# First-layer weights in two transfers of 2 KB rows, keys' powers on GpSimd, and a last transposition ahead of its logits

## The chip, the cores and the metric

The kernel runs on one core of one Trainium2 chip. A core has a matmul engine (TensorE, PE in the profile, with its weight loads listed as PEld), VectorE (DVE), ScalarE (ACT), GpSimd (POOL) and SyncE (SP). In this kernel SP issues nearly all transfers between HBM and the on-chip memory, and 16 DMA engines carry them out. The metric is the time of one execution in microseconds of device time; lower is better. The profile is one execution recorded by the hardware profiler.

## The reference

The first part is a linear attention with decay over q, k and v of shape (4, 8, 768, 64). It is computed in blocks of 64 positions with a running state per head:

```python
for b in range(nb):
    intra = np.einsum('bhic,bhjc->bhij', qb, kb) * Dmask[None]
    intra = np.einsum('bhij,bhjd->bhid', intra, vb)
    inter = np.einsum('bhid,bhde->bhie', qb * lam_pow[None], kv_state)
    out[:, :, sl] = intra + inter
    kb_dec = kb * rev_pow[None]
    kv_state = lam_block[None, :, None, None] * kv_state + np.einsum('bhsd,bhse->bhde', kb_dec, vb)
```

`Dmask`, `lam_pow` and `rev_pow` are powers of one decay per head. The second part is a soft mixture of experts over the 3072 rows x of that output (512 wide), with 8 experts of 4 slots each:

```python
logits = x @ phi                       # 3072 x 32
d = softmax of logits over the rows    # dispatch
slot_input = d.T @ x                   # 32 slots x 512
h = np.maximum(slot_input[e] @ w1[e], 0.0)   # 512 x 1024 per expert
slot_out[e] = h @ w2[e]                      # 1024 x 512 per expert
c = softmax of logits over the slots   # combine
return c @ slot_out
```

All data are float32. The two weight tensors have 16.8 MB each.

## The kernel before, in words

**Chunks.** The 3072 rows are worked through in T = 24 chunks of 128 rows (6 to a batch element), in a Python loop that writes out every instruction. Each engine runs its own instructions in the order written; a helper records every operation, so that the profile puts all of them on line 52, and one tells them apart by tile names. For chunk t:

- `scores(t)`: PE multiplies keys by queries into the banks `sc0` and `sc1`; DVE multiplies by the decay `mask` into `at`.
- `recall(t)`: PE multiplies the running state `st` by the decayed queries `qs` into the banks `xa` and `xb`.
- `turn_k(t + 1)`: for chunks whose natural-order keys are not loaded, PE transposes `kT` of the next chunk and ACT copies it to `kn`.
- `natural(t - 1)`: PE transposes the finished chunk `xt` into `tr`, ACT copies it to `x`.
- `attend(t)`: PE adds `at` times v into `xa` and `xb`, which are copied to `xt`; then ACT swaps the halves of the next chunk's v into `vs`.
- `state(t)`: PE multiplies the decayed keys `kd` by v into `kv`; DVE adds it to the decayed state.
- `decay_q(t + 1)` and `decay_k(t + 1)`: POOL makes `qs` and `kd` for the next chunk. `kd` needs the keys' powers `kp`.

Every fourth chunk adds the logits of four finished chunks (`logits`, bank `gl`, with a running maximum and an exponential `e` on ACT) and, a chunk later, their contribution to the slot inputs (`slots`, into `acc`).

**Loads.** SP issues the loads in program order. At chunk t it issues qT and kT of chunk t + 2, then as many first-layer tiles as a fixed pace gives (`load_early`; tile `slab`, 128 partitions x 2 x 512), then vN and, where wanted, kN of chunk t + 2. The chunk loads have 256 KB each and go round 10 buffers; a slab has 512 KB, one row of 4 KB per partition, and there are 35 slab buffers: 32 for the first layer w1, and the first ones of w2 (`w2p`, two rows of 2 KB per partition). The rest of w2 is loaded where buffers of the chunk phase come free (`w2t`, 256 KB) and into used slabs (`w2p`). Program order puts kT of chunk 3 behind 2 slabs, kT of chunk 12 behind 16, and kT of chunk 21 behind 30.

**Start.** DVE builds `mask` by scans; in chunk 0 ACT swaps v (`swap_v(0)`), copies the powers out of the mask (`key_powers`), and PE runs a few warm-up matmuls on a tile of zeros (into `dp`).

**The bridge.** After the last chunk, `attend(23)` leaves `xt` in two halves, one copied by ACT and one by DVE. The logits of that chunk (`pr`, bank `sc0`) are then multiplied on PE, DVE takes their maximum (`mx`, `nm`), ACT takes the weight `wgt` of what came before (tile `alpha`) and the exponentials `el` (tile `e`), POOL makes `selw` from the weight, and PE transposes `e`. The last chunk is also transposed to natural order (`tr`, copied to `xl`, tile `x`), and `slots` of the last group is done. All of it goes into the slot inputs (`si`, bank `xb`), and with that the expert layers start: `first(0)`, `first(1)` with the slabs, then `second` with w2, between whose parts the output is combined and stored.

The pace at which slabs are issued is set by these lines:

```python
asked = sum(3 + loaded(x) for x in range(min(t + 3, T)))
want = max(sent, min(NSLAB, (AHEAD + (t + 1) * PACE - 10 * asked) // 20))
load_early(want - sent)
```

Of the kernel before, what the change touches and what calls it, by code (L numbers as in the profile page):

```python
# [8 lines left out]
F32 = mybir.dt.float32  # L9
F32R = mybir.dt.float32r  # L10
AF = mybir.ActivationFunctionType
# [3 lines left out]
P = 128  # L15
B, H, S, DH = 4, 8, 768, 64
NB = S // P
T = B * NB
HP = H // 2
D = H * DH  # L20
# [8 lines left out]
HD = D // 2  # L29
# [7 lines left out]
def loaded(t):  # L37

    return t == 0 or t % NB in (2, 4)
# [18 lines left out]
def decay_attn_soft_moe(  # L58
# [13 lines left out]
    pe, dve, act, pool, sp = (InOrder(tc, x) for x in (nc.tensor, nc.vector, nc.scalar, nc.gpsimd, nc.sync))  # L72
# [5 lines left out]
    keep = ctx.enter_context(tc.tile_pool(name="keep", bufs=4))  # L78
    small = ctx.enter_context(tc.tile_pool(name="small", bufs=2))
# [5 lines left out]
    def bank(tag):  # L85
        return SC.get(tag) or ps.tile([P, 512], F32, tag=tag, name=tag)
# [7 lines left out]
    def load_chunk(t, which=(0, 1, 2, 3)):  # L94
        srcs = (qT, kT, vN, kN)
        for i in which:
            if i == 3 and not loaded(t):
                continue
            tl = loads.tile([P, 512], F32, tag="ld", name="ld")
            sp.dma_start(out=tl, in_=srcs[i][t])  # L100
            IN[t, i] = tl
# [13 lines left out]
    def load_one(pool_, tag, bufs):  # L115
        Q, f, q = late.pop()
        t_ = pool_.tile([P, 512], F32, tag=tag, name="w2t", bufs=bufs)
        sp.dma_start(out=t_, in_=w2[4 * Q + q, f])
        wt["w2", Q, q, f] = t_

    def load_two():

        (Q, f, q), _ = late.pop(), late.pop()
        t_ = slabs.tile([P, 2, 512], F32, tag="slab", name="w2p")
        sp.dma_start(out=t_, in_=w2[4 * Q + q:4 * Q + q + 2, f].rearrange("e p d -> p e d"))
        for i in range(2):
            wt["w2", Q, q + i, f] = t_[:, i, :]

    def load_early(n):
        for _ in range(n):  # L130
            if early:
                _, Q, kc, q = early.pop()
                t_ = slabs.tile([P, 2, 512], F32, tag="slab", name="slab")
                sp.dma_start(out=t_, in_=w1[4 * Q + q, kc])
                wt["w1", Q, q, kc] = t_
            else:
                load_two()
# [9 lines left out]
    def warmup(n):  # L147
        for _ in range(n):
            pe.matmul(out=wps[:, 0:P], lhsT=warm[:, P:2 * P], rhs=warm[:, P:2 * P], start=True, stop=True)
# [5 lines left out]
    ident = const.tile([P, P], F32, name="ident")  # L155
# [16 lines left out]
    mask = work.tile([P, 2, HP, P], F32, tag="mask", name="mask")  # L172
    for hh in range(2):
        for hp in range(HP):
            x = hh * HP + hp

            dve.tensor_tensor_scan(
                out=mask[:, hh, hp, :],
# [21 lines left out]
    kp = small.tile([P, 2, HP, 1], F32, tag="kp", name="kp", bufs=1)  # L200
    kpow = kp.rearrange("p a b o -> p (a b) o")

    def key_powers():
        act.copy(out=kp[:, :, 0:2], in_=mask[:, :, 0:2, P - 1:P])
        for i in range(2):
            act.copy(out=kp[64 * i:64 * i + 64, :, 2:HP], in_=mask[64 - 64 * i:P - 64 * i, :, 2:HP, P - 1:P])

    CN = const.tile([P, T, SL], F32, name="CN")
    acc = const.tile([P, D], F32, name="acc")
# [4 lines left out]
    def load_phi():  # L214

        sp.dma_start(out=e.rearrange("p (k s) -> p k s", k=4), in_=phi)
# [10 lines left out]
    AT, XT, X, ST, QS, KD = {}, {}, {}, {}, {}, {}  # L227
# [192 lines left out]
    def weights(raw=True):  # L420
        dp = bank("dp")
        pe.transpose(dp[:, 0:P], e, ident)
        if raw:
            pe.transpose(dp[:, P:2 * P], L, ident)
        dve.tensor_copy(out=d, in_=dp[:, 0:P])
        return dp[:, P:2 * P]
# [57 lines left out]
    for t in range(T):  # L484
        if t + 2 < T:
            load_chunk(t + 2, (0, 1))
# [4 lines that stand above are left out]
        sent = max(sent, want)  # L491
        if t + 2 < T:
            load_chunk(t + 2, (2, 3))
        if t == 1:
            load_phi()

        for _ in range((2, 4, 3)[t - T + 3] if t >= T - 3 else 0):
            load_one(*ld1)
        if t == T - 1:
            load_one(work, "kd", 1)  # L500
            load_one(work, "kn", 1)
        last = t == T - 1

        asks = t // 4 - 1 if t > 0 and t % 4 == 0 else G - 1 if last else None
        sums = t // 4 - 1 if t > 4 and t % 4 == 1 else None
        scores(t)
        if t == 0:
            swap_v(0)
            key_powers()
            warmup(2)  # L510

        if t % 4 == 3 or t % 4 == 0:
            next(sm, None)
        if t == T - 1:
            next(sm, None)
        opens = t % NB == 0
        if t == 0:
            decay_k(0)
            powers()
            decay_q(1)  # L520
        recall(t)
        if sums is not None:
            sm = slot_softmax(sums, weights())
        if t > 0:
            if not opens:
                turn_k(t + 1)
            natural(t - 1)
        if sums is not None:
            next(sm)
        if asks is not None:  # L530
            ask = logits(asks)
            next(ask)
        if last:
            next(ask)

            phi4 = [
                work.tile([P, 2, 4, SL], F32, tag=tg, name="phi4", bufs=n) for tg, n in (("dec", 1), ("st", 2))
            ]
            for i in range(2):
                two = phi_sb[:, 2 * i:2 * i + 2].rearrange("p (a o) s -> p a o s", o=1)  # L540
                pool.tensor_copy(out=phi4[i], in_=two.broadcast_to([P, 2, 4, SL]))
        if opens and t > 0:

            state(t)
        attend(t)
        if t == 0:
            state(0)
            turn_k(1, "tr")
        if last:
            weights(raw=False)  # L550
            cm = bank("kv")
            pe.matmul(out=cm[:, 0:4], lhsT=blk_, rhs=gm, start=True, stop=True)
            dve.tensor_reduce(out=own, in_=cm[:, 0:4], axis=AX.X, op=ALU.min)
        if t == 0:
            dve.tensor_reduce(out=sel, in_=ident.rearrange("p (g s) -> p s g", g=4), axis=AX.X, op=ALU.add)
            for Q in range(2):
                rows = bass.AP(tensor=ident.tensor, offset=ident.offset + 16 * Q, ap=[ident.ap[0], [36, 4], [1, NR]])
                dve.tensor_reduce(out=own2[:, Q:Q + 1], in_=rows, axis=AX.XY, op=ALU.add)
            dve.tensor_reduce(out=gsel, in_=ident.rearrange("p (g s) -> p g s", g=4), axis=AX.X, op=ALU.add)
        if opens and t > 0:  # L560
            turn_k(t + 1)
        if t > 0:
            decay_q(t + 1)
        if not opens:
            state(t)
        decay_k(t + 1)
        if asks is not None and not last:
            next(ask)
        if sums is not None:
            slots(sums)  # L570
        if t == 2:
            place_phi()
        if t == 3:
            pool.tensor_copy(out=blk, in_=sel.rearrange("p (o s) -> p o s", o=1).broadcast_to([P, 4, SL]))
# [4 lines left out]


    negm = run["m"]
    pr = bank("sc0")
    for hp in range(HP):
        pe.matmul(
            out=pr[:, 0:P],
# [7 lines left out]
    dve.tensor_reduce(out=mx, in_=pr, axis=AX.X, op=ALU.max)  # L593
    new = small.tile([P, 1], F32, tag="nm", name="nm")
    dve.scalar_tensor_tensor(out=new, in0=mx, scalar=-1.0, in1=own, op0=ALU.mult, op1=ALU.min)
    tr = bank("tr")
    for hp in range(HP):
        pe.transpose(tr[:, hp * P:(hp + 1) * P], XT[T - 1][:, hp, :], ident)
    xl = keep.tile([P, D], F32, tag="x", name="x", bufs=5)
    act.copy(out=xl[:, 0:HD], in_=tr[:, 0:HD])  # L600
    dve.tensor_copy(out=xl[:, HD:D], in_=tr[:, HD:D])
    wgt = small.tile([P, 1], F32, tag="alpha", name="alpha")
    act.activation(out=wgt, in_=negm, func=AF.Exp, bias=new, scale=-1.0)
    el = e
    rs = small.tile([P, 1], F32, tag="rs", name="rs")
    act.activation(out=el, in_=pr, func=AF.Exp, bias=new, scale=1.0, accum_out=rs)
    selw = small.tile([P, SL], F32, tag="selw", name="selw", bufs=1)
    pool.tensor_scalar(out=selw, in0=sel, scalar1=wgt, scalar2=None, op0=ALU.mult)
    for half in range(2):
# [7 lines left out]
    for first_, (w_, x_) in ((True, (selw, acc)), (False, (dn, xl))):  # L617
        for kc in range(4):
            pe.matmul(
                out=si[SL * kc:SL * kc + SL, 0:P],  # L620
# [242 lines left out]
```

## Time and profile before

| | |
|---|---|
| median of 3 runs | 167.2 us (166.39 to 169.53) |
| the profiled execution | 166.92 us, span 165.1 us |
| busy: PE, PEld, DVE, ACT, POOL | 145.9, 104.5, 93.1, 81.0, 65.8 us |
| moved by DMA | 61.56 MB, mean 373 GB/s |
| first matmul of the first expert layer | 116.15 us |
| last matmul on the chain that ended last | about 155.6 us |

The span runs from the first to the last recorded instruction. The profile gives each engine's busy time; the waits (which instruction stood idle, and what released it); the timeline (start, duration, engine, operation, output and inputs, how many are merged in one line, and in brackets the idle time before it with its releaser); the DMA issues (kind, count, KB, and the time from issue to landing); and the DMA queues (packets, MB, and the share of 16 engines' time). "issue" in brackets means that the engine waited for nothing that the profile shows. PE is busy in most of the span, and the 16 DMA engines are busy in nearly all of it.

### The profile page before, as it was taken

The page shows a single profiled execution, that of the slowest core. Times are in us where ns is not written, and L with a number is a line of the kernel's source. Part 1 is how long each engine was busy: PE and PEld are TensorE (multiplying, and loading weights), DVE is VectorE, ACT ScalarE, POOL GpSimd, SP SyncE. Part 2 cuts the span into 40 slices and gives each one's busy share as a digit, 9 for nine tenths or more (in the row PEclk, how much of TensorE's full clock was granted, in tenths as well). Part 3 has the DMA queues.
Part 4 walks back from the last instruction along what each step waited for, and adds up shares of the span by engine and source line. Part 5 has one row for each costly group of instructions (what it writes and reads, how often), then busy time and mean ns, then how long its engine had stood idle before and what let it go on. Part 6 is the DMA issues. An engine that isn't in the chain of part 4 may idle for free. (4 is left out here: it accounts for less than half of the span.)

```text
span 165.1 us, 6357 instructions
## 1 busy us (share of the span) xinstructions
PE 145.9 (88%) x2633; PEld 104.5 (63%) x2633; DVE 93.1 (56%) x218; ACT 81.0 (49%) x203; POOL 65.8 (40%) x93
## 2 busy tenths in 40 slices
PE   6788977999999979998999999998999999999800
PEld 6567866678796857686767888775233345456600
DVE  4984433458475546449265848586118799345800
ACT  3445645457365646565475746542010698333800
POOL 2188592227766107658322766710000285000000
PEclk9999999999999999999999999999999999999965
DMA  5999999999999999999999999998999999998895
GB/s 171 350 406 404 414 405 410 410 406 408 401 349 395 412 409 404 414 329 354 396 396 402 391 383 377 333 311 325 358 397 408 409 401 408 400 370 301 310 384 199
DMA packets 32012, 61.56 MB, mean 373 GB/s; under 512 B 3056, under 2 KB 9328, under 8 KB 31984
## 3 DMA queue, kind: packets, MB, share of 16 engines
q1 hardware_dynamic: 31840, 61.16, 98.7%
q8 instruction: 21, 0.34, 0.8%
q14 instruction: 7, 0.06, 0.1%
q10 hardware_dynamic: 144, 0.01, 0.1%
HBM read 54.86 MB, written 6.29 MB: 370 GB/s over the span
## 5 line engine op out<-in xcount | busy, mean ns | idle before, releaser
L52 DVE TENSOR_TENSOR at<-sc,mask 128x512 f32<-128x512 f32 x48 | 30.9, 685 | 13.0 <-PE sc L52 12.6
L52 POOL TENSOR_TENSOR qs<-ld,qpow 128x512 f32<-128x512 f32 x20 | 25.6, 1279 | 2.0 <-POOL kd L52 1.3
L52 ACT COPY x<-tr 128x512 f32<-128x512 f32 (+1 forms) x24 | 13.9, 579 | 22.7 <-PE tr L52 22.7
L52 PE MATMUL sc<-ld 64*64 64x128 f32 (+1 forms) x768 | 22.7, 252 | 2.4 <-issue 2.4
L52 PEld LDWEIGHTS sc<-ld 64*64 64x64 f32 x768 | 18.9, 134 | 9.0 <-issue 3.4
L52 ACT COPY vs<-ld 64x256 f32<-64x256 f32 x48 | 19.4, 403 | 5.1 <-DMA ld<-vN 4.3
L52 POOL TENSOR_TENSOR dec<-st,qpow 128x256 f32<-128x256 f32 x16 | 9.9, 621 | 24.8 <-DVE st L52 24.8
L52 POOL TENSOR_TENSOR kd<-kn,kp 128x512 f32<-128x512 f32 x11 | 11.5, 1043 | 15.2 <-ACT kn L52 15.2
L52 DVE TENSOR_TENSOR st<-dec,kv 128x256 f32<-128x256 f32 x16 | 6.7, 420 | 16.9 <-PE kv L52 15.6
L52 PE MATMUL tr<-ident,xt 128*128 128x128 f32 x96 | 15.3, 281 | 0.0
L52 PE MATMUL xa<-qs,st 64*64 64x128 f32 x160 | 13.4, 277 | 1.5 <-issue 1.0
L52 PE MATMUL kv<-ld,kd 128*64 128x64 f32 x320 | 13.2, 223 | 0.8 <-POOL kd L52 0.8
L52 PE MATMUL xb<-qs,st 64*64 64x128 f32 x160 | 13.7, 279 | 0.0
L52 PEld LDWEIGHTS kv<-ld,kd 128*64 128x64 f32 x320 | 12.0, 138 | 1.7 <-POOL kd L52 1.1
L52 POOL TENSOR_TENSOR kd<-ld,kp 128x512 f32<-128x512 f32 x9 | 9.6, 1068 | 6.1 <-ACT kp L52 6.1
L52 PEld LDWEIGHTS tr<-ident,xt 128*128 128x128 f32 x96 | 10.6, 141 | 2.1 <-issue 1.9
L52 ACT COPY kn<-kv 128x512 f32<-128x512 f32 x10 | 5.9, 585 | 11.9 <-PE kv L52 11.9
L52 PE MATMUL xa<-at,ld 128*64 128x128 f32 x96 | 10.4, 295 | 1.1 <-DVE at L52 1.1
L52 PEld LDWEIGHTS xa<-qs,st 64*64 64x64 f32 x160 | 9.0, 133 | 2.2 <-issue 1.3
L52 PE MATMUL xa<-at,vs 128*64 128x128 f32 x96 | 9.6, 273 | 0.3 <-issue 0.3
L52 PE MATMUL xb<-at,vs 128*64 128x128 f32 x96 | 9.6, 273 | 0.0
L52 PE MATMUL xb<-at,ld 128*64 128x128 f32 x96 | 9.5, 274 | 0.0
(152 smaller groups left out, 265.4 us busy)
## 6 DMA issues: line engine op xcount, KB each, us to landing
slab<-w_x SPq DMA_DIRECT2D x32, 512.0 KB, 6.8
w2p<-w_x SPq DMA_DIRECT2D x20, 512.0 KB, 9.2
ld<-qT SPq DMA_DIRECT2D x24, 256.0 KB, 5.9
ld<-kT SPq DMA_DIRECT2D x24, 256.0 KB, 5.9
ld<-vN SPq DMA_DIRECT2D x24, 256.0 KB, 6.8
w2t<-w_x SPq DMA_DIRECT2D x24, 256.0 KB, 5.3
y<-o SPq DMA_DIRECT2D x24, 256.0 KB, 3.5
ld<-kN SPq DMA_DIRECT2D x9, 256.0 KB, 5.8
```

Source lines behind the costliest of these rows:

```text
L52: return self._tc.keep_in_program_order(f(*args, **kwargs))
```

## The change

1. Each first-layer tile is loaded by two transfers of 256 KB, one for each half of the row of a partition (2 KB each), instead of one of 512 KB with rows of 4 KB. The order among the loads is kept.
2. The three small copies that gather the keys' powers go from ACT to POOL, and 4 instead of 2 warm-up matmuls run in chunk 0.
3. In the last chunk, DVE's copy of the logits to `L` and its update of `lsum` (the second step of `logits`) come behind `attend` instead of ahead of it.
4. After the last chunk, its four transpositions and the two copies to `xl` come ahead of its logits instead of behind their maximum; the exponentials `el` come ahead of the weight `wgt` on ACT.

```diff
@@ load_early
                 t_ = slabs.tile([P, 2, 512], F32, tag="slab", name="slab")
-                sp.dma_start(out=t_, in_=w1[4 * Q + q, kc])
+                for i in range(2):
+                    sp.dma_start(out=t_[:, i], in_=w1[4 * Q + q, kc][:, i])
                 wt["w1", Q, q, kc] = t_
@@ key_powers
-        act.copy(out=kp[:, :, 0:2], in_=mask[:, :, 0:2, P - 1:P])
+        pool.tensor_copy(out=kp[:, :, 0:2], in_=mask[:, :, 0:2, P - 1:P])
         for i in range(2):
-            act.copy(out=kp[64 * i:64 * i + 64, :, 2:HP], in_=mask[64 - 64 * i:P - 64 * i, :, 2:HP, P - 1:P])
+            pool.tensor_copy(out=kp[64 * i:64 * i + 64, :, 2:HP], in_=mask[64 - 64 * i:P - 64 * i, :, 2:HP, P - 1:P])
@@ the loop over chunks
             key_powers()
-            warmup(2)
+            warmup(4)
...
         if last:
-            next(ask)
 ...
             state(0)
             turn_k(1, "tr")
         if last:
+            next(ask)
             weights(raw=False)
@@ after the loop
     negm = run["m"]
+    tr = bank("tr")
+    for hp in range(HP):
+        pe.transpose(tr[:, hp * P:(hp + 1) * P], XT[T - 1][:, hp, :], ident)
+    xl = keep.tile([P, D], F32, tag="x", name="x", bufs=5)
+    act.copy(out=xl[:, 0:HD], in_=tr[:, 0:HD])
+    dve.tensor_copy(out=xl[:, HD:D], in_=tr[:, HD:D])
     pr = bank("sc0")
...
     dve.scalar_tensor_tensor(out=new, in0=mx, scalar=-1.0, in1=own, op0=ALU.mult, op1=ALU.min)
-    tr = bank("tr")
-    for hp in range(HP):
-        pe.transpose(tr[:, hp * P:(hp + 1) * P], XT[T - 1][:, hp, :], ident)
-    xl = keep.tile([P, D], F32, tag="x", name="x", bufs=5)
-    act.copy(out=xl[:, 0:HD], in_=tr[:, 0:HD])
-    dve.tensor_copy(out=xl[:, HD:D], in_=tr[:, HD:D])
-    wgt = small.tile([P, 1], F32, tag="alpha", name="alpha")
-    act.activation(out=wgt, in_=negm, func=AF.Exp, bias=new, scale=-1.0)
     el = e
     rs = small.tile([P, 1], F32, tag="rs", name="rs")
     act.activation(out=el, in_=pr, func=AF.Exp, bias=new, scale=1.0, accum_out=rs)
+    wgt = small.tile([P, 1], F32, tag="alpha", name="alpha")
+    act.activation(out=wgt, in_=negm, func=AF.Exp, bias=new, scale=-1.0)
```

## The prediction

> **What bounds the kernel now.** I read the page's busy times, the DMA issues, the chain that ended last, then the waits of SP and of the weight loads, and the timelines around the lines that change.
>
> ```profile
> PE 145.9 (88%) x2633; PEld 104.5 (63%) x2633; DVE 93.1 (56%) x218; ACT 81.0 (49%) x203; POOL 65.8 (40%) x93
> q8 instruction: 21, 0.34, 0.8%
> slab<-w_x SPq DMA_DIRECT2D x32, 512.0 KB, 6.8
> ld<-kT SPq DMA_DIRECT2D x24, 256.0 KB, 5.9
> w2t<-w_x SPq DMA_DIRECT2D x24, 256.0 KB, 5.3
> 116.15 1.07 PE gl L52 x8
> ```
>
> The last row is the chain's first matmul of the first expert layer. From there the chain is PE, piece upon piece without a wait, until 152.1 us; then come the last copies and stores. So the end moves with the moment at which the first layer starts, and an edit counts by what it does to the 24 chunks before 116 us or to the bridge at 111 to 116 us.
>
> In the chunks PE is nearly full, yet it stops in the middle of runs of equal matmuls:
>
> ```profile
> 23.03 0.30 PEld L52 LDWEIGHTS sc<-ld 64*64 64x64 f32 x12 [1.11 <-issue]
> 29.22 0.42 PEld L52 LDWEIGHTS sc<-ld 64*64 64x64 f32 x16 [1.43 <-issue]
> 60.40 0.70 PEld L52 LDWEIGHTS gl<-xt,phi_sb 128*32 128x32 f32 x27 [1.24 <-issue]
> 78.74 0.13 PEld L52 LDWEIGHTS xa<-qs,st 64*64 64x64 f32 x1 [1.28 <-issue]
> q8 instruction: 1, 0.02, 5.5%
> ```
>
> Nothing that the profile shows releases these. The queue row is of the stretch 26.7 to 27.7 us: in it one block of a program was fetched, in 5.5% of 16 engines for 1.0 us = 0.9 us, and PE went on 1.5 us after it, at 29.22. The page counts 2 x 2633 PE instructions and 21 blocks, 251 to a block. I read the stalls as PE at the end of a block with the next one not there. If a block is asked for when PE enters the one before (my inference), the block fetched from 26.7 us was asked for at 23.03 and stood 3.7 us in line, behind what SP had issued.
>
> How much stands in line is set by SP, which issues a transfer only when an earlier one has landed:
>
> ```profile
> 9.11 0.33 SPq L52 DMA_DIRECT2D ld<-kT  x1
> ld<-kT SPq DMA_DIRECT2D x1, 256.0 KB, 6.6
> 15.75 0.33 SPq L52 DMA_DIRECT2D ld<-vN  x1
> SPq L52 <- DMA slab<-w_x: 10.9, 15, 0.9
> ```
>
> This kT lands at 9.11 + 6.6 = 15.7; the vN issued right then is the eighth transfer after it. So eight are in flight, whatever their size, and splitting a slab puts fewer bytes in line.
>
> **The change part by part.**
>
> *The split, as DMA work.* The first two rows are of 26.7 to 27.7 us, where slabs alone are moved, the third of 132 to 138 us, where all rows have 2 KB, the fourth of 20.6 to 21.7.
>
> ```profile
> DMA packets 108, 0.42 MB, mean 416 GB/s; under 512 B 8, under 2 KB 8, under 8 KB 107
> q1 hardware_dynamic: 107, 0.40, 99.2%
> q1 hardware_dynamic: 1251, 2.41, 104.4%
> q1 hardware_dynamic: 229, 0.42, 100.5%
> ```
>
> A 4 KB packet takes 16 x 1.0 x 0.992 / 99 = 160 ns. A 2 KB packet takes 16 x 6 x 1.044 / 1179 = 85 ns without the small ones. A slab has 128 of the first; two halves have 256 of the second: (170 - 160) x 128 / 16 = 0.08 us more per slab, 2.6 us for 32. By the mixed stretch a 2 KB packet takes 16 x 1.1 x 1.005 / 201 = 88 ns: 0.13 us per slab, 4.1 us in all. I take 0.08, from the longer stretch. SP issues 32 more transfers at about 0.33 us, 11 us of its own time, while it waits for landings anyway.
>
> Does a later load stop PE? The tightest places are the transpositions of kT for chunks 3, 12 and 21:
>
> ```profile
> 15.81 0.41 PE L52 MATMUL kv<-ident,ld 128*128 128x128 f32 x2 [0.63 <-DMA ld<-kT]
> 47.39 0.48 SPq L52 DMA_DIRECT2D ld<-kT  x1
> ld<-kT SPq DMA_DIRECT2D x1, 256.0 KB, 7.1
> 55.56 0.42 PEld L52 LDWEIGHTS kv<-ident,ld 128*128 128x128 f32 x4 [0.17 <-issue]
> 88.34 0.42 SPq L52 DMA_DIRECT2D ld<-kT  x1
> ld<-kT SPq DMA_DIRECT2D x1, 256.0 KB, 5.6
> 95.56 0.31 PEld L52 LDWEIGHTS kv<-ident,ld 128*128 128x128 f32 x3 [0.17 <-issue]
> ```
>
> Chunk 3: PE waits already, and 2 slabs stand ahead: +0.16 us, at once. Chunk 12: landed at 54.5, used at 55.56, margin 1.1, against 16 slabs x 0.08 = 1.3. Chunk 21: landed at 93.9, used at 95.56, margin 1.6, against 30 x 0.08 = 2.4. The DMA engines have slack to give back where SP stood waiting for a buffer:
>
> ```profile
> 45.00:50.00 5.00, 5.00 (x118) 4.45 (x118) 3.19 (x10) 3.31 (x11) 2.86 (x3) 1.00 0.96 348
> 70.00:75.00 5.00, 5.00 (x112) 4.25 (x104) 2.93 (x6) 2.67 (x7) 3.11 (x4) 1.00 0.94 335
> 75.00:80.00 5.00, 3.97 (x96) 3.29 (x96) 3.41 (x8) 2.19 (x6) 3.66 (x5) 1.00 1.01 371
> 135.00:140.00 5.00, 5.00 (x99) 2.99 (x92) 4.85 (x12) 4.85 (x13) 3.38 (x9) 1.00 1.05 408
> ```
>
> The last column is GB/s. The fourth row is a full stretch, of 2 KB rows alone. Against its 408 the first lost 5 x 60 / 408 = 0.7 us, the others 0.9 and 0.45. So the loads could be 0.7 us earlier by chunk 12 and 2.1 by chunk 21.
>
> *The split, as a shorter line.* Eight transfers of 256 KB take what the w2t take, 5.3 us to land, against 5.9 to 6.8 now; I put the line 1.1 us shorter. That taken off the first three stalls leaves 0.0, 0.3 and 0.1 us, a gain of 1.1 + 1.1 + 1.1 = 3.3. The fourth falls in the stretch 75 to 80 us, where the engines weren't full, so the line was short already; I leave it whole. But what is late next is the loads. PE can be ahead by 1.1 + 0.7 - 1.3 = 0.5 us at chunk 12, and by 1.6 + 2.1 - 2.4 = 1.3 at chunk 21, if the slack is given back; a PE that is ahead frees its buffers earlier, so it is. After chunk 21 no kT is as near its use. I take the 1.3 us. The bounds for the split: all four stalls gone, a gain of 5.1; or the line unchanged and all DMA work at its upper price on the path, a loss of 4.1.
>
> The Trainium skill ("Runtime: NRT & Kernel Launch", section on instruction fetch mechanics) says that instructions come in blocks of 16 KiB, which its sequencer fetches by a DMA queue of its own, and that crossing a boundary is mostly hidden. The trace agrees on the size (0.34 MB in 21 blocks) and not on the hiding: 1.11 to 1.43 us are shown. By that sentence the stalls would be something else and the gain nothing.
>
> *Keys' powers.*
>
> ```profile
> 7.13 0.61 ACT L52 COPY kp<-mask 128x4 f32<-128x4 f32 x3
> 7.82 1.26 POOL L52 TENSOR_TENSOR kd<-ld,kp 128x512 f32<-128x512 f32 x1 [6.06 <-ACT kp L52]
> 9.76 1.27 POOL L52 TENSOR_TENSOR qs<-ld,qpow 128x512 f32<-128x512 f32 x1 [0.68 <-DVE qpow L52]
> L52 POOL COPY d<-ident 128x64 f32<-128x64 f32 x2 | 0.4, 236 | 0.0
> ```
>
> ACT's three copies, 0.61 us, stand behind its swap of v. POOL waits for them (6.06 us) with nothing else to do, and would need up to 3 x 236 ns = 0.7 us, as they are smaller than that row's: the decayed keys start earlier by what ACT spends on the swap, less 0.1. But POOL's next step waits for DVE's powers until 9.76 in any case, and chunk 3 waits for its load. So 0; without this cover it would be 0.1 slower to 0.8 faster. The two extra warm-up matmuls lie where PE waits for DVE's first `at`, and shift the block ends by a few instructions: 0.
>
> *The bridge.*
>
> ```profile
> 111.21 0.29 DVE L52 COPY L<-gl 96x128 f32<-96x128 f32 x1
> 111.77 1.13 PE L52 MATMUL sc<-xt,phi 128*128 128x128 f32 x8
> 113.37 0.37 ACT L52 COPY x<-tr 128x256 f32<-128x256 f32 x1 [1.75 <-PE tr L52]
> 113.83 0.36 ACT L52 ACTIVATE e<-sc,nm 128x128 f32<-128x128 f32 x1
> 114.03 0.37 POOL L52 TENSOR_SCALAR selw<-sel,alpha 128x32 f32<-128x32 f32 x1 [5.55 <-ACT alpha L52]
> 115.12 0.32 PE L52 MATMUL xb<-acc,selw 128*32 128x128 f32 x4 [0.45 <-DVE dn L52]
> ```
>
> Four transpositions ahead of the eight logits put these 4 x 1.13 / 8 = 0.55 us later in PE's queue. About 0.3 is made good: DVE's part of `xt` no longer stands behind the copy of `L` (0.29). Against the rest, `x` is copied while the logits run, so that ACT is free for `e` when the new maximum comes, and does it ahead of the weight's exponential: `e` some 0.1 us earlier than 113.83. DVE has no copy of `x` left between the maximum and its two `acc` updates. The weight comes after `e`, so `selw` ends near 113.73 + 0.36 + 0.36 + 0.37 = 114.8 (the weight's exponential taken as long as `e`), and PE goes on near 114.9 instead of 115.12. I take -0.2 us; -0.5 if `selw` isn't last, +0.3 if the logits' delay stays.
>
> **Sum.** The 0.16 at chunk 3 is within the 2.4 of the later margin and isn't added. -1.3 - 0.2 = -1.5 us against the profiled execution's 166.9 (a span of 165.1 and 1.8 around it): 165.4. The median of the runs shown, 167.2, is 0.3 above it, so 165.7. A measurement of this kernel can tell about 2%, 3.3 us, from no change.
>
> **Rivals.**
>
> *The line isn't shorter.* The fetch queue may be served between loads, and the stalls have another cause. For it: the 1.28 us stall stands where few slabs were in flight. Against it: the fetch at 26.7 us, 3.7 after the stall that should have triggered it. Then PE keeps its stalls, SP's waits hide the 2.6 us, chunk 3 costs 0.16 and the bridge gives 0.2: 167.2. Chance 0.30. The Trainium skill ("DMA: Bandwidth & Descriptors", section on queues, rings and completion order) has each DMA engine take turns between queues at every packet, which speaks for this rival.
>
> *Loads become the bound (slower).* The halves' source rows lie 4 KB apart, which the trace shows for no load. If a slab costs c more, chunk 21 is pushed by 30c against 1.6 + 2.1 = 3.7 us: it decides from c = 0.12. By the mixed stretch's 0.13 this is 30 x 0.13 - 3.7 = +0.2 us. At twice that, 0.25, it is +3.8, or 171.0, and slower by 2%. Nothing in the rows has such a price, so the middle: c = 0.19, +2.0, 169.2. Chance 0.13, half of it beyond 2%.
>
> *The stalls go whole.* If the loads have more slack than I found, the 3.3 us count, with the bridge's 0.2: 167.2 - 3.5 = 163.7; with the fourth stall, 162.4. For it: the three stretches with slack come after chunk 10 and the price of a slab is small. Against it: chunk 12's 0.5 us. Chance 0.14.
>
> **Numbers.** The forecast has 0.43, with 164.5 to 166.7 as its own range. Range 163.3 to 168.6: it leaves out a third of the whole-gain case and most of the slow one. 2% is reached below 163.9 and above 170.5. Faster by over 2%: most of the 0.14 and a little of the forecast, 0.17. Slower: 0.08. Within: 0.75.
>
> **What would show it.** Slab halves of 256 KB landing in about 5.3 us, and ld in the same; PEld's waits for issue on `sc`, `xa` and `gl` down by 2 us or more; new PE waits for ld near chunks 9 to 12; the first `kd` starting ahead of 7.82; the logits' exponential ahead of the weight's and some 0.1 us earlier against the first logit matmul's old place. I am wrong if the stalls keep their length, or if windows at 10 to 45 us fall well under 400 GB/s.

## The result, and the profile after

The changed kernel takes 168.87 us (median of 20 runs, 165.98 to 173.04), the kernel before 166.8 (20 runs, 164.47 to 172.53): 1.0122 of it, with an interval of 1.0082 to 1.0162. That is slower, by 2.07 us at the medians, where 1.5 us of gain was forecast. Executions over 1.5% above the fastest of their kernel are left out of each ratio, so that it need not be the quotient of the medians; the profiled ones of the changed kernel, of the split alone, of the rows of 2 KB and of the even and odd partitions are among those left out. The profiled execution of the changed kernel took 169.25 us (span 167.5).

First, of the changed kernel, the issues of slabs and kT (count, KB, us to landing), and from the chain the first matmul of the first layer.

```profile
slab<-w_x SPq DMA_DIRECT2D x64, 256.0 KB, 5.5
ld<-kT SPq DMA_DIRECT2D x24, 256.0 KB, 5.3
118.48 1.07 PE gl L52 x8
```

The first layer starts at 118.48 us in place of 116.15. From there to the end it is 169.25 - 118.48 = 50.77 us, and before 166.92 - 116.15 = 50.77. So all of the loss was made ahead of the first layer, as the prediction's first step has it. The windows from 8 us to that start, of before and then of after, split it (PE busy is the second number, the last two are the DMA share and GB/s):

```profile
8.00:116.15 108.15, 100.40 (x2165) 81.00 (x2161) 62.71 (x149) 58.83 (x153) 57.40 (x64) 1.00 1.02 386
```
```profile
8.00:118.48 110.48, 101.25 (x2168) 82.08 (x2164) 62.60 (x150) 59.09 (x153) 56.46 (x64) 0.98 1.03 380
```

PE stands idle for 110.48 - 101.25 = 9.23 us against 7.75 before, 1.48 more, and it is busy 0.85 us longer, at a mean clock of 0.98. What it waits for has changed. Waits of 8 to 96 us, before and after (sum, count, longest), of the matmuls (PE) and of the weight loads (PEld):

```profile
PE sc L52 <- issue: 2.4, 3, 1.3
PE xa L52 <- issue: 1.3, 2, 1.0
PE gl L52 <- issue: 1.1, 1, 1.1
PEld sc L52 <- issue: 3.2, 5, 1.4
PEld xa L52 <- issue: 3.1, 10, 1.3
PEld gl L52 <- issue: 2.3, 7, 1.2
```
```profile
PE kv L52 <- DMA ld<-kT: 3.8, 2, 2.0
PE kv L52 <- issue: 0.7, 1, 0.7
PE sc L52 <- issue: 0.2, 1, 0.2
PEld xa L52 <- issue: 1.4, 7, 0.3
PEld gl L52 <- issue: 1.0, 6, 0.2
PEld sc L52 <- issue: 0.8, 4, 0.3
```

The stalls that the prediction puts down to program blocks, up to 1.4 us each, are gone from `sc`, `xa` and `gl`: what the weight loads still wait there is at most 0.3 us. One of 0.7 us stands on `kv`, at 84.19 us. The matmuls' idle time without a visible cause falls from 2.4 + 1.3 + 1.1 = 4.8 us to 0.9. In its place PE waits for kT, 3.8 us instead of one wait of 0.6, and 0.9 more just behind 96 us. The timeline of after at chunks 3, 15 and 21:

```profile
9.90 0.33 SPq L52 DMA_DIRECT2D ld<-kT  x1
16.79 0.81 PE L52 MATMUL kv<-ident,ld 128*128 128x128 f32 x4 [2.03 <-DMA ld<-kT]
71.07 0.63 PE L52 MATMUL kv<-ident,ld 128*128 128x128 f32 x4 [1.77 <-DMA ld<-kT]
96.69 0.52 PE L52 MATMUL kv<-ident,ld 128*128 128x128 f32 x3 [0.92 <-DMA ld<-kT]
```

The loads are late, and SP shows that it is mostly not for want of a buffer. Its waits over the whole span, before and after: buffers come free when POOL is done with a chunk's keys (`kd`) or PE with its matmuls (`kv`), and SP waits for those far less; for the landing of a slab it waited 10.9 us in 15 waits before.

```profile
SPq L52 <- POOL kd L52: 10.4, 7, 1.8
SPq L52 <- PE kv L52: 9.1, 9, 1.8
```
```profile
SPq L52 <- DMA slab<-w_x: 16.7, 50, 1.8
SPq L52 <- PE kv L52: 2.4, 7, 0.8
SPq L52 <- POOL kd L52: 1.4, 1, 1.4
```

### The profile page after: what moved, and what is told of

It is laid out like the page before. It is cut to its first block, busy times and chain, and to the rows that moved or that the text cites. A ratio compares the mean times of both kernels' runs of the same rounds, so it can differ in the third digit from the quotient of the medians.

```text
span 167.5 us, 6407 instructions
## 1 busy us (share of the span) xinstructions
PE 147.8 (88%) x2637; PEld 106.8 (64%) x2637; DVE 93.2 (56%) x218; ACT 80.4 (48%) x200; POOL 66.4 (40%) x96
## 4 chain that ended last, share of the span: by engine, by line
PE 53%; DMA 27%; POOL 5%; issue 5%; DVE 4%; DVEq 0%; ACT 0%; SPq 0%; POOLq 0%; ACTq 0%
PE xa L52 11%; DMA slab<-w_x 11%; PE kv L52 10%; PE sc L52 7%; PE tr L52 7%; DMA ld<-kN 7%; PE gl L52 6%; PE xb L52 6%; DMA ld<-kT 6%; PE dp L52 5%; DMA ld<-vN 3%; POOL qs L52 2%; DMA y<-o 1%; POOL dec L52 1%; POOL kd L52 1%
## 5 line engine op out<-in xcount | busy, mean ns | idle before, releaser
L52 PE MATMUL xb<-qs,st 64*64 64x128 f32 x160 | 13.2, 280 | 0.0
L52 PE MATMUL kv<-ident,ld 128*128 128x128 f32 x40 | 6.7, 288 | 5.4 <-DMA ld<-kT 4.7
L52 ACT COPY xt<-xa 128x256 f32<-128x256 f32 x24 | 8.8, 368 | 2.8 <-PE xa L52 2.7
```

The source lines that it names most:

```text
L52: return self._tc.keep_in_program_order(f(*args, **kwargs))
```

## The experiments

The line is, as in the prediction, what SP has issued and what has not landed yet. Three theories were set against each other. A: eight transfers of 256 KB hold too few bytes in line, and the DMA engines lose rate. B: the 2 KB packets cost more than was priced. C: the other parts of the change cost the time.

### The parts of the change apart

**The split alone.**

```diff
-                sp.dma_start(out=t_, in_=w1[4 * Q + q, kc])
+                for i in range(2):
+                    sp.dma_start(out=t_[:, i], in_=w1[4 * Q + q, kc][:, i])
```

> The kernel before with the split alone. Theory A (eight transfers of 256 KB are too few bytes in flight: one DMA engine that falls behind holds up the issue of the next loads): about 1.2% slower, as the whole change. Theory B (the price of 2 KB packets, 0.08 us for each slab): also about 1.2% slower. Theory C (the copies on GpSimd, the warm-up or the bridge cost the time): no change.

168.75 us (6 runs), 1.018 of before (1.009 to 1.027): the split alone costs as much as the whole change. Windows, first of before, then of the split alone, with the DMA rate last:

```profile
8.00:46.00 38.00, 34.02 (x759) 28.07 (x755) 19.80 (x43) 20.46 (x52) 22.91 (x27) 1.00 1.04 406
46.00:96.00 50.00, 47.29 (x1028) 38.03 (x1027) 30.00 (x67) 28.55 (x73) 25.83 (x27) 1.00 1.02 388
```
```profile
8.00:46.00 38.00, 33.71 (x738) 27.27 (x736) 18.47 (x44) 19.45 (x49) 22.19 (x27) 1.00 1.02 372
46.00:96.00 50.00, 46.71 (x1035) 37.67 (x1034) 28.89 (x65) 28.51 (x76) 25.05 (x26) 1.00 1.04 385
```

By 46 us, at 372 GB/s in place of 406, the loads are 38 x (406 / 372 - 1) = 3.5 us behind; in the changed kernel, with 385, it is 38 x (406 / 385 - 1) = 2.1 us. The prediction allowed 16 x 0.08 = 1.3 us there. From 46 to 96 us, where the prediction had them give 2.1 us back, the rate is below that of before as well, though the DMA engines are full (1.04).

**All but the split** (whole slabs; powers on GpSimd, warm-up and bridge as changed), in two studies.

```diff
-                for i in range(2):
-                    sp.dma_start(out=t_[:, i], in_=w1[4 * Q + q, kc][:, i])
+                sp.dma_start(out=t_, in_=w1[4 * Q + q, kc])
```

> All of the change but the split: slabs in one transfer with rows of 4 KB. Theories A and B: 0.2 us faster, or no difference that can be measured. Theory C: about 1.2% slower.

> All of the change but the split (whole first-layer tiles; keys' powers on GpSimd, two more warm-up matmuls, the bridge's new order), a second time and with more rounds. If the split is the whole loss, this is within 0.5% of the kernel before (by the prediction's 0.2 us for the bridge, 0.999), and the wait of PE for kT stays at 0.6 us. If the other parts cost something of their own (theory C), 1.01 comes back.

166.22 us (6 runs), 1.011 (1.004 to 1.017); then 168.17 us (12 runs), 1.003 (0.997 to 1.009). The one median is below that of before (166.8) and the other above (166.68); with the second interval across 1, neither a cost nor a gain of these parts is established. Added to the alternate split, below, they change nothing either (0.993 and 0.992).

### Rows, partitions and depth in the kernel

**One transfer of 512 KB with rows of 2 KB** (halves stored apart in HBM, so that a partition gets two packets).

```diff
+                sp.dma_start(out=t_, in_=w1[4 * Q + q, kc].rearrange("i p d -> p i d"))
```

> The kernel before, with each slab in one transfer of 512 KB, its halves stored apart in HBM so that the packets have 2 KB. The count of transfers and the bytes in flight are those of before, the packets those of the change. Theory A: no change, slabs landing in about 6.8 us. Theory B: about 1.2% slower (2 us).

167.54 us (12 runs), 1.009 (1.004 to 1.014). Theory A had no change, theory B 1.012.

```profile
8.00:46.00 38.00, 34.89 (x748) 29.03 (x746) 19.49 (x44) 20.17 (x49) 22.04 (x27) 1.00 1.05 401
```

PE's wait for kT from 8 to 96 us is that of before again, one of 0.6 us, and the rate is 401. So the packets, with a full line behind them, cost about half of the split's loss by the middle values (the intervals overlap), and don't bring about the 372.

**Two transfers of 256 KB with rows of 4 KB**, on the even and the odd partitions.

```diff
+                for i in range(2):
+                    sp.dma_start(out=t_[i::2], in_=w1[4 * Q + q, kc][i::2])
```

> The kernel before, with each slab in two transfers of 256 KB with rows of 4 KB, the even partitions and the odd ones. Count, size and bytes in flight are those of the change, the packets those of before, and unlike with two halves of the partitions the rows are spread over all of them. Theory A: 0.5 to 1% slower (the whole change less the packets). Theory B: no change.

172.32 us (6 runs), 1.032 (1.024 to 1.041).

```profile
8.00:46.00 38.00, 33.18 (x732) 27.23 (x732) 18.76 (x43) 19.74 (x48) 22.04 (x27) 1.00 1.02 379
```

Large packets don't help here, which speaks against B alone, and the loss is larger than the 0.5 to 1% of A. The stride over partitions may cost something of its own; that was not taken apart. Four whole slabs, below, are the short line without it.

**Two transfers of 64 partitions each**, with rows of 4 KB.

```diff
+                for i in range(2):
+                    sp.dma_start(out=t_[64 * i:64 * i + 64], in_=w1[4 * Q + q, kc][64 * i:64 * i + 64])
```

> The kernel before, with each slab in two transfers of 64 partitions each, rows of 4 KB. The same count and size of transfers as in the change, but with the packets of before. Theory A: about 1.2% slower (2 us), with the loads' time to land at 5.0 to 5.5 us. Theory B: no change.

218.01 us (6 runs), 1.315 (1.302 to 1.328). It was meant to show depth alone, and doesn't, since such transfers are slow in themselves:

```profile
8.00:46.00 38.00, 27.50 (x532) 21.36 (x530) 13.77 (x32) 14.39 (x36) 15.27 (x20) 0.91 1.01 266
```

### Transfers by themselves

For the rate alone, a kernel that loads the 32 slabs twice into 24 buffers, with or without matmuls beside it; all other work is left out.

```diff
+    for rep in range(2):
+        for n in range(32):
+            t_ = slabs.tile([P, 2, 512], F32, tag="slab", name="slab")
+            sp.dma_start(out=t_, in_=src)                       # whole
+            for i in range(2):                                   # or halves
+                sp.dma_start(out=t_[:, i], in_=src[:, i])
+    for n in range(1000):                                        # or 4
+        pe.matmul(out=acc[0:64, 0:64], lhsT=z[:, 0:64], rhs=z[:, 64:128], start=True, stop=True)
```

**Whole slabs and 1000 small matmuls; halves and 1000; halves and 4.**

> Only transfers and a PE that waits for none of them: 64 slabs of 512 KB in whole transfers with 4 KB rows (the first-layer weights twice), beside 1000 small matmuls on a tile of zeros; the attention and the experts are left out and the output is zeros. Theory A: above 420 GB/s while the slabs are moved (4 KB packets at 160 ns, engines full), and PE, which needs a new block of program every 5 us, stalls at each by more than 2 us, since the block stands behind eight slabs.

> The same with each slab in two halves of 256 KB with 2 KB rows. Theory A: well under 400 GB/s, since an engine that fetches a block of program falls behind and eight transfers of 256 KB don't cover it; PE's stalls shorter by more than half. Theory B (only the price of packets): 400 GB/s or more, with the engines as full as with whole slabs.

> The halves again, with 4 matmuls in place of the 1000, so that PE fetches no program beside the transfers. Theory A: 400 to 410 GB/s, as nothing makes one engine fall behind. If eight transfers of 256 KB are too few by themselves, it is as slow as with the 1000 matmuls.

The windows of 20 to 60 us of the three, in this order:

```profile
20.00:60.00 40.00, 40.00 (x690) 40.00 (x688) 0.00 (x0) 0.00 (x0) 1.00 1.03 408
```
```profile
20.00:60.00 40.00, 40.00 (x690) 40.00 (x688) 0.00 (x0) 0.00 (x0) 1.00 1.03 371
```
```profile
20.00:60.00 40.00, 0.00 (x0) 0.00 (x0) 0.00 (x0) 0.00 (x0) 1.00 1.05 387
```

Whole executions: 122.24, 123.26 and 109.47 us, one of each, as for all kernels of this section. Halves lose rate twice: 408 to 387, and beside the matmuls to 371. Neither forecast for the third, 400 to 410 or as slow as the second, came.

PE's forecast stalls of more than 2 us at each block didn't come: PE is busy for 40.00 of 40.00 us beside whole slabs, each of which takes 10.2 us to land. A block lasts about 251 x 40 / (690 + 688) = 7.3 us here. If it is asked for when PE enters the one before, as the prediction infers, it came in less than that, and so doesn't stand behind the whole line. These kernels show what fetches cost the loads; what the line costs a fetch, only the full kernels show.

**One transfer of 512 KB with rows of 2 KB, and four whole slabs under way in place of eight** (both with 1000 matmuls).

```diff
-            sp.dma_start(out=t_, in_=src)
+            sp.dma_start(out=t_, in_=src.rearrange("i p d -> p i d"))    # rows
...
-    slabs = ctx.enter_context(tc.tile_pool(name="slabs", bufs=24))
+    slabs = ctx.enter_context(tc.tile_pool(name="slabs", bufs=4))        # depth
```

> Transfers alone and 1000 small matmuls, as in the earlier stream of whole slabs (the rest of the work is left out); but each transfer of 512 KB has two rows of 2 KB per partition, 64 KB and more apart in HBM. Bytes in flight as with whole slabs, packets as with halves. Theory A: 404 to 408 GB/s between 20 and 60 us, landing 10 us. Theory B (the price of 2 KB packets): 371 GB/s, as the halves had.

> The same stream with whole slabs of 4 KB rows, but only four slab buffers, so that four transfers of 512 KB are under way and not eight: 2 MB in flight as with halves, packets as with whole slabs, half as many transfers. Theory A: 371 GB/s between 20 and 60 us, as eight halves had, and a slab lands in 5.4 us. Theory B: 408 GB/s, since the packets are of 4 KB.

```profile
20.00:60.00 40.00, 40.00 (x690) 40.00 (x688) 0.00 (x0) 0.00 (x0) 1.00 1.05 387
```
```profile
20.00:60.00 40.00, 40.00 (x689) 40.00 (x688) 0.00 (x0) 0.00 (x0) 1.00 1.00 369
```

(123.42 and 122.26 us.) A misses the first of the two, B both. The rows of 2 KB cost 408 to 387 with a full line: 524 / 387 - 524 / 408 = 0.07 us per slab. Without matmuls halves had these 387 too, so that a short line alone is no loss. Beside them a line of 2 MB costs the rest, with either packet: 371 and 369. Four whole slabs show when. The page's view of DMA queues for 15 to 17.5 us, then windows of this kernel:

```profile
q8 instruction: 1, 0.02, 2.4%
```
```profile
13.00:16.00 3.00, 3.00 (x55) 3.00 (x54) 0.00 (x0) 0.00 (x0) 1.00 1.01 414
17.00:18.00 1.00, 1.00 (x20) 1.00 (x19) 0.00 (x0) 0.00 (x0) 1.00 0.72 270
18.00:19.00 1.00, 1.00 (x21) 1.00 (x20) 0.00 (x0) 0.00 (x0) 1.00 0.76 291
23.00:24.00 1.00, 1.00 (x21) 1.00 (x19) 0.00 (x0) 0.00 (x0) 1.00 1.04 426
```

A program block is fetched in 2.4% x 16 x 2.5 = 1.0 us of one DMA engine's time; the engines' share then falls to 0.72 to 0.76 for two us and comes back. Not every fetch costs the same: the stream of halves keeps 386 GB/s from 20 to 34 us with two fetches in it, and has 331 from 34 to 42 us, under the same matmuls.

**Halves beside 70 wide matmuls; whole slabs and halves by turns beside 1000 small ones.** The first keeps PE busy almost without fetches.

```diff
-        pe.matmul(out=acc[0:64, 0:64], lhsT=z[:, 0:64], rhs=z[:, 64:128], start=True, stop=True)
+        pe.matmul(out=acc, lhsT=z[:, 0:128], rhs=z, start=True, stop=True)   # 70 of these, halves
...
-            if MODE == "whole":
+            if MODE == "whole" and n % 2:                                     # by turns
```

> The stream of halves (rest of the work left out), but beside 70 matmuls of 128 x 512 in place of 1000 small ones: TensorE stays busy for most of 20 to 60 us with under 250 instructions, so hardly a program block is fetched in it. If the fetches make the short line run dry, 387 GB/s comes back, as without matmuls. If it is TensorE's activity, about 371.

> The stream beside 1000 small matmuls, with whole slabs and halves by turns (rest left out): packets half 4 KB, half 2 KB, eight transfers of 384 KB on average in flight. By the packets alone the rate is the middle of 408 and 387, 397 GB/s. If 3 MB in line are enough beside the fetches it is that, 395 to 398; if not, 375 to 390.

Window and fetches (20 to 60 us) of the wide matmuls, the fetches beside 1000 small ones with halves, and the window of the slabs by turns:

```profile
20.00:60.00 40.00, 40.00 (x95) 17.72 (x94) 0.00 (x0) 0.00 (x0) 1.00 1.05 386
q8 instruction: 1, 0.02, 0.2%
```
```profile
q8 instruction: 5, 0.08, 0.8%
```
```profile
20.00:60.00 40.00, 40.00 (x689) 40.00 (x688) 0.00 (x0) 0.00 (x0) 1.00 1.04 397
```

(110.21 and 122.74 us.) With PE as busy, and 1 fetch in place of 5, halves have their 387 back. In the stream of halves the small matmuls run as evenly where the rate is kept (244 from 20 to 34 us) as where it is lost (141 from 34 to 42), so that the loss goes with the fetches, if not with every one, and not with PE's activity. With slabs by turns the rate is the middle of 408 and 387, 397.5: a line of 3 MB loses nothing to five fetches. How a fetch costs rate is argued, not shown. That the other engines run dry while one is held fits the share behind the fetch above, but over 20 to 60 us it is only part: with four whole slabs the share is 1.00 against 1.03, 3% less, and the rate 369 against 408, 10% less, so that packets also took longer. The trace does not name the engine of a packet.

### Every second slab split

```diff
-                sp.dma_start(out=t_, in_=w1[4 * Q + q, kc])
+                if len(early) % 2:
+                    sp.dma_start(out=t_, in_=w1[4 * Q + q, kc])
+                else:
+                    for i in range(2):
+                        sp.dma_start(out=t_[:, i], in_=w1[4 * Q + q, kc][:, i])
```

> The kernel before with every second first-layer tile split: eight transfers in flight hold about 3 MB in place of 4 (whole) or 2 (halves). Theory A (rate set by what is in flight): the DMA rate between 8 and 46 us lies between 406 and 372 GB/s, nearer the upper (a reserve that is larger than one landing's delay), PE's stalls for program blocks lie between those of the kernel before (7.6 us) and of the split alone (3.6), and the time is between 0.995 and 1.01 of the kernel before. Rival (any split slab costs its price, whatever is in flight): half of the split's loss, 1.009.

164.39 us (12 runs, 163.35 to 166.3) against 166.68 in the same study: 0.992 of before (0.988 to 0.996). Its windows and its largest waits for a block and for kT (8 to 96 us):

```profile
8.00:46.00 38.00, 34.95 (x793) 29.04 (x788) 20.12 (x47) 21.36 (x55) 22.23 (x28) 1.00 1.05 404
46.00:96.00 50.00, 48.45 (x1046) 38.96 (x1045) 30.48 (x68) 28.81 (x73) 27.52 (x28) 1.00 1.04 401
8.00:113.67 105.67, 100.01 (x2166) 80.78 (x2161) 62.38 (x150) 58.77 (x153) 56.62 (x64) 1.00 1.04 395
```
```profile
PEld sc L52 <- issue: 2.3, 5, 0.9
PE kv L52 <- DMA ld<-kT: 0.9, 1, 0.9
```

The time is a little below the 0.995 that theory A allowed, and the rival's 1.009 falls. The rate is kept (404), the stalls for blocks are shorter (0.9 at most on `sc`, in place of 1.4), and PE stands idle for 5.66 us in place of 7.75 ahead of the first layer, which starts at 113.67. The 401 in place of 388 from 46 to 96 us is no gain of this split: the two profiles of all but the split, with whole slabs, have 398 and 400 there, and their idle times ahead of the first layer are 6.66 and 7.35 us. So it is shown that the rate is kept; where the gain of 0.8% comes from is shown only in part.

**The same with all other parts of the change.**

> Every second first-layer tile split, together with all other parts of the change. If the others are worth nothing that can be measured, as their two runs alone say (1.011 and 1.003 of the kernel before), this has the time of the alternate split alone, 0.99 of before within 0.5%. If the prediction's 0.2 us at the bridge counts, 0.1% less.

164.59 us (12 runs), 0.993 (0.988 to 0.997), as the alternate split alone. Both are faster than the kernel before by under 1%; neither beats the other. They were not measured beside the kernel after, which has 1.0122 of before.

## Why the prediction was wrong

- **The end follows the first layer's start**: right, 50.77 us behind it in both.
- **Eight in flight, a shorter line, shorter stalls**: right. A kT lands in 5.3 us in place of 5.9, a slab in 5.5 in place of 6.8, and the longest stalls for a block on `sc`, `xa` and `gl` fell from 1.2 to 1.4 us to 0.2 to 0.3. PE's own idle time of this kind fell by 4.8 - 0.9 = 3.9 us, where 3.3 was forecast. That the stalls are block ends, which the prediction inferred, has support in the trace of before: among PE's recorded matmuls and weight loads they stand at the 693rd, 945th, 2205th and 2959th, 252, 1260 and 754 apart, which is 1, 5 and 3 blocks of 251. How much of the fall is the shorter line and how much is PE coming later, held up by kT, was not taken apart; the alternate split, where PE waits little for kT, still has stalls of up to 0.9 us.
- **0.08 us per slab for the packets**: right by the stream, 0.07. In the kernel with a full line even that costs 1.009; there a slab takes 6.9 us to land, no less than before, and no stalls are saved.
- **The step that failed is the DMA slack, and with it the price of a slab.** The sum priced packets only, and took the 408 GB/s of 135 to 140 us as the rate whatever the line. In that stretch the queue view shows no fetch, and the transfers had 512 KB and landed in 10.2 us. Beside fetches a line of halves has 371: 524 / 371 - 524 / 408 = 0.13 us per slab, just above the 0.12 from which the prediction's own slow rival decides. And the 2.1 us were not given back: from 46 to 96 us the kernel after moves 381 GB/s with full engines (1.03), less than the 388 of before with its pauses, so that there was no slack below 408 to use. With both terms put right, the prediction's sum for chunk 21 is 1.6 + 0 - 30 x 0.13 = -2.3 us, an estimate near the 2.07 us of loss. By 46 us the loads of the kernel after are 2.1 us behind, which is 16 x 0.13; those of the split alone are 3.5 behind, more than this price gives. So where 1.1 + 1.1 + 1.1 us of stalls went, PE waited 2.0, 1.8 and 0.9 us for kT.
- **Chunk 3, +0.16**: a term too small. kT is issued at 9.90 in place of 9.11, and lands 6.5 us later by its own row in place of 6.6: 0.7 us later, and PE, which is there 0.4 us earlier than before (14.76 in place of 15.18), goes on 0.98 us later (16.79 in place of 15.81). Two more transfers stand ahead of it, and places in flight are counted in transfers, where the prediction counted bytes. The places looked at were chunks 3, 12 and 21; after the change PE waits at 3, 15 and 21.
- **Keys' powers, 0**: nothing to be seen in the time. With the copies on POOL `kd` starts at 6.99 us (after), with those on ACT at 7.27 (split alone): 0.28 us sooner, and kT of chunk 3 is what PE waits for afterwards.
- **The bridge, -0.2**: wrong in sign, +0.23. The last `attend` matmuls and the exponential behind them, before and after:

```profile
110.48 0.16 DVE L52 SCALAR_TENSOR_TENSOR nm<-mx,nm 96x1 f32<-96x1 f32 x1
110.72 0.39 PE L52 MATMUL xb<-at,vs 128*64 128x128 f32 x4
110.73 0.36 ACT L52 ACTIVATE e<-gl,nm 96x128 f32<-96x128 f32 x1 [1.03 <-PE xa L52]
```
```profile
112.64 0.15 DVE L52 SCALAR_TENSOR_TENSOR nm<-mx,nm 96x1 f32<-96x1 f32 x1
112.82 0.39 PE L52 MATMUL xb<-at,vs 128*64 128x128 f32 x4
113.17 0.36 ACT L52 ACTIVATE e<-gl,nm 96x128 f32<-96x128 f32 x1 [1.36 <-PE xb L52]
```

  From that `xb` to the first layer it is 116.15 - 110.72 = 5.43 us before and 118.48 - 112.82 = 5.66 after. The other profiles agree: 5.43 to 5.44 us in the four with the old order (the split alone, the rows, the even and odd partitions, the alternate split), 5.60 to 5.68 in the three with the new one. The exponential starts 0.53 us behind `nm` in place of 0.25; the trace puts it down to `xb`, a wait that the forecast did not look for. From the transposition of `e` (`dp`) on, the bridge is 4.81 us (113.67 to 118.48) in place of 4.92 (111.23 to 116.15): there the forecast's order works, by half of what it gave.
- **The rivals.** "The line isn't shorter" (0.30) falls with the landings. "Loads become the bound" (0.13) is what happened, at 168.87 where it said 169.2. So close a number is in part luck: that rival took 0.19 us per slab and let the 2.1 us of slack stand, and the runs show 0.13 and no slack; the source rows 4 KB apart, by which it argued, show no price of their own: halves without fetches have 387 GB/s, as rows 64 KB apart have. "The stalls go whole" (0.14) was wrong for this split. The alternate split, with three quarters of the line, has 0.992 of before, where that rival's 163.7 is 163.7 / 167.2 = 0.979: part of such a gain was there, at another length of the line.

## What to carry to other kernels

What stands in line has two readers: a short line lets urgent transfers and program blocks through sooner, and a long one kept the rate of the loads through the fetches. When a transfer is split, look up both, and try the lengths in between; here 2 MB lost rate beside the fetches, 4 MB kept it with the long stalls, and 3 MB had the rate of the one and part of the short stalls of the other. Take the rate of a full line from a stretch with the same fetches and the same bytes in flight, count transfers as well as bytes ahead of an urgent load, and look at every such load rather than at three.

## What was not expected of the hardware

**TensorE's clock.** In the profile of after, the wait for kT of chunk 3 was followed by half the clock (the last three numbers are the clock, the DMA share and GB/s):

```profile
17.00:18.00 1.00, 1.00 (x7) 1.00 (x6) 0.00 (x0) 0.31 (x1) 0.64 (x1) 0.58 1.05 385
20.00:21.00 1.00, 1.00 (x24) 0.93 (x24) 0.00 (x0) 0.57 (x2) 0.00 (x0) 0.71 1.08 342
```

PE was idle for 2.03 us, and the clock stayed near 0.5 for some 3.4 us (17.2 to 20.6 by these shares). Two more profiles have such a stretch of 3.4 us: that of the rows of 2 KB behind an idle time of 1.86 us (from 79.3 us), and that of the even and odd partitions behind one of 2.24 (from 101.5). A wait of 1.77 us in the profile of after, and those of 1.2 to 1.4 in the split alone, left the clock at 1.00. It can explain the 0.85 us that PE is busy longer in this profile, but not the loss itself: the split alone is as slow without it. No run took this wait away by itself. The Trainium skill ("TensorE: Matmul & The Clock Gate", section "Part 1: The HAM clock gate") gives half rate after an idle window of some 3.4 us and a window as long until full rate. The length of the slow stretch agrees with it; the idle times ahead of it here, 1.86 to 2.24 us, are shorter.

**Halves of the partitions.** Transfers of 64 partitions moved 266 GB/s at a DMA share of 1.01, where whole ones moved 406 at 1.04: on the mean of all loads in that window, a byte keeps an engine busy 406 x 1.01 / (266 x 1.04) = 1.48 times as long. The Trainium skill ("DMA: Bandwidth & Descriptors", section "Rules for kernel authors") advises against transfers of disjoint partition halves, since they serialize; this run shows more than that, a third less rate and 1.315 of the time. Why was not taken apart.
